# More word and stage places for the conversion of the second layer's inputs, home loads two positions apart, and other rules for the activation's jobs

## The chip, the core and the metric

One core of a Trainium2 chip. The metric is the device time of one execution in microseconds. Five engines work beside each other, each through its own queue in order: TensorE (PE, with its weight loads PEld), VectorE (DVE), ScalarE (ACT), GpSimd (POOL) and SyncE (SP). DMAs are issued here on SP's and ACT's queues.

## What is computed

An attention with feature maps (4 batches, 8 heads, 576 rows, 64 columns), whose output is laid out as 2304 tokens of 512, and then two layers of two products each. The second layer's inputs, and the first layer's weights, come as 64-bit floats.

```python
h = x @ w_in            # first layer: 2304 x 512 by 512 x 2048
g = np.maximum(0.01 * h, h)
x = (g @ w_out)         # 2048 x 512
h = x @ w_in            # second layer, weights of its own
sp = np.where(h > 20.0, h, np.log1p(np.exp(np.minimum(h, 20.0))))
g = h * np.tanh(sp)
out = (g @ w_out)
```

## The kernel before

The program runs through five stages: attention (to 180 us), the first layer's first product (to 352), its second product (352 to 575), the second layer's first product (575 to 772), and the last product (772 to 981). Every fp32 product is made of three matmuls (`three`, L97 to L100) on a high and a low part: `split` (L93 to L95) makes the high part on ScalarE (L94) and the low part on VectorE (L95). The second product of a layer runs in 72 steps of 12 matmuls, TensorE's operands being the weights at their *home* and the activations *gh*, *gl* (first layer) or *g* (second layer).

Beside TensorE's work a **planner** issues all other work. It is written in the kernel (`Stage`, `Chain`, `Lane`, `work`): each call of `work` is one *position*. It adds `rate` to a budget of VectorE time, and lets each active chain make its next stage if its gate is free, its places are there (`ok`), the stage before it is `after` positions old, and the budget is above zero. In the two second products a position stands behind each half step, so two positions to a step and six matmuls to a position. `work(True)` is a forced round, which looks neither at the budget nor at the age of a stage.

**Conversion of inputs.** 64-bit weights are loaded raw into a *stage* place (512 KB), and turned into fp32 on VectorE (L182, L184, L169, L197) and ScalarE (L190), in *word* places. `w2_chain` converts two such units of the second layer's input weights and stores their sums and parts to DRAM (`pd`, L1070); `to_parts` does it for a unit of its output weights (`po`, L985). A unit can only begin when a stage place has been loaded and two word places are open. In the first layer's second product the planner has two stage places and four word places; the tiles `s8` to `s13` of the first layer's inputs are out of use there until the second layer's inputs are made. In the last chunk of that product the code waits for the conversions:

```python
            if m == 3:
                free.add("u3")
                while any(x.tile is not None for x in places.stages) or loads.at < len(loads.units):
                    work(True)
```

It stands behind step 3 of the last 16 steps, with TensorE's next matmuls behind it in the program.

**The activation of the second layer** is done in 36 *jobs* (`job`, 128 x 1024 each): load `job<-hp` (L1370), exp (L1378), u, n (L1382, L1385), ln, exp (L1388, L1391), t1, t2 (L1394), t3 (L1405), t4 (L1409), store `gp<-job` (L1414). All but exp and ln are VectorE's. Jobs run in the lane `jobs`, four at a time, in tiles of the pool `wide`. They begin in the second layer's first product and go on to the end of the last one. `Pairs` loads their results as *raw* tiles (L1446) into three places in turn (`st0`, `st1`, `cc`), which until then serve jobs (`wide_at`, closed by `gates2`), and splits them: pair q, of 36, stands behind the first half of step 2q - 2 and is read from step 2q on.

**Home loads.** `to_home` loads the 16 last weights (`wo<-po`, 512 KB each, L1292) from DRAM to their homes. Eight wait for the gate `s0`, six for `s1`, two for `c1`; they are 16 chains, so those of a gate go at one position.

## Time and profile before

| | us |
|---|---|
| median of 3 runs | 986.84 (986.5 to 987.19) |
| the profiled execution | 987.44 |
| its span in the trace | 985.4 |
| TensorE busy | 927.7 (94%) |
| VectorE busy | 746.8 (76%) |
| ScalarE busy | 562.8 (57%) |
| GpSimd busy | 68.7 (7%) |
| DMA, whole span | 221.38 MB, 225 GB/s |

The time of the profiled execution is its span and 2.0 us around it. The page cuts the span into 40 slices of 24.6 us: a digit is the busy share in tenths, and PEclk the granted clock of TensorE in tenths of full speed. In the list of waits the engine and line that waited stand left of the arrow, what ended the wait right of it. In a timeline, a number in brackets is the idle time ahead of the instruction and what ended it.

### The profile page before, as it was taken

The numbers are of one execution on the slowest core, as the hardware profiler recorded it, in microseconds if no ns is written. First come the engines' busy times: TensorE is split into PE (matmuls) and PEld (weight loads), VectorE is DVE, ScalarE is ACT, GpSimd is POOL, SyncE is SP. The second block draws the span as 40 slices with busy tenths as digits, with TensorE's granted clock in tenths as the row PEclk, the third lists the DMA queues.
The fourth block names the chain that finished last, engine by engine and source line by source line (L and its number), as shares of the span: only waits on it lengthen the run. The fifth ranks groups of instructions, "written<-read, shape, count | busy, mean of one in ns | idle before, by whom it ended". The sixth has DMA issues, their size and how long they took to land.

```text
span 985.4 us, 17037 instructions
## 1 busy us (share of the span) xinstructions
PE 927.7 (94%) x6549; PEld 783.6 (80%) x6549; DVE 746.8 (76%) x1100; ACT 562.8 (57%) x869; POOL 68.7 (7%) x36
## 2 busy tenths in 40 slices
PE   8999999999999999999992899999999599999998
PEld 7899999788888888889881688787877488887886
DVE  7888987588888337776767696777877388888894
ACT  6788888555666445454443465464655346654461
POOL 3434442000000000000000000000000000000000
PEclk9999999999999999999996899999999899999999
DMA  7425521279887777887878646887888948565743
GB/s 202 132 75 143 140 61 31 101 237 308 301 284 263 259 233 236 268 282 255 266 249 266 242 155 226 288 294 267 303 284 309 415 161 298 192 236 192 237 169 128
DMA packets 126416, 221.38 MB, mean 225 GB/s; under 512 B 33664, under 2 KB 58624, under 8 KB 126336
## 3 DMA queue, kind: packets, MB, share of 16 engines
q1 hardware_dynamic: 89312, 144.40, 44.1%
q10 hardware_dynamic: 37024, 75.91, 22.0%
q8 instruction: 51, 0.84, 0.4%
q14 instruction: 29, 0.24, 0.1%
HBM read 131.66 MB, written 88.60 MB: 224 GB/s over the span
## 4 chain that ended last, share of the span: by engine, by line
PE 53%; DVE 14%; DMA 7%; issue 6%; ACT 6%; ACTq 0%; SPq 0%; DVEq 0%
PE a L98 8%; PE b L98 8%; PE a L100 8%; PE b L99 8%; PE b L100 8%; PE a L99 8%; DVE job L1394 3%; DVE job L1385 2%; DVE job L1405 2%; DMA wo<-po 2%; DVE g L95 2%; ACT job L1388 2%; DMA hp<-g 1%; DVE job L1409 1%; ACT job L1391 1%
## 5 line engine op out<-in xcount | busy, mean ns | idle before, releaser
L1394 DVE SCALAR_TENSOR_TENSOR job<-job 128x1024 f32<-128x1024 f32 x72 | 88.0, 1223 | 43.2 <-ACT job L1391 42.5
L1388 ACT ACTIVATE job<-job,two 128x1024 f32<-128x1024 f32 x36 | 41.5, 1152 | 93.8 <-DVE job L1385 91.3
L95 DVE TENSOR_TENSOR gl<-raw,gh 128x512 fp32r<-128x512 f32 x72 | 49.6, 691 | 59.6 <-ACT gh L94 56.4
L98 PE MATMUL b<-gh,wo 128*128 128x512 f32 (+1 forms) x192 | 68.9, 359 | 21.1 <-ACT gh L94 21.1
L94 ACT ACTIVATE gh<-raw 128x512 fp32r<-128x512 f32 x72 | 44.9, 627 | 62.0 <-PE a L100 15.7
L95 DVE TENSOR_TENSOR g<-raw,g 128x1024 fp32r<-128x1024 f32 x36 | 44.0, 1222 | 42.2 <-ACT g L94 40.8
L444 POOL PARTITION_ALL_REDUCE qm<-qd x32 | 68.5, 2188 | 91.0 <-ACT qd L439 82.3
L99 PE MATMUL b<-gl,wo 128*128 128x512 f32 (+1 forms) x192 | 69.0, 359 | 2.7 <-DVE gl L95 2.7
L98 PE MATMUL b<-wo,g 128*128 128x512 f32 x160 | 63.3, 395 | 6.7 <-ACT g L94 6.7
L100 PE MATMUL b<-gh,wo 128*128 128x512 f32 (+1 forms) x192 | 68.7, 358 | 0.0
L98 PE MATMUL b<-win,w 128*128 128x512 f32 x128 | 52.5, 410 | 12.3 <-DVE g L831 7.5
L100 PE MATMUL b<-wo,g 128*128 128x512 f32 x160 | 63.4, 396 | 0.5 <-DVE g L95 0.4
L99 PE MATMUL b<-wo,g 128*128 128x512 f32 x160 | 63.0, 394 | 0.0
L98 PEld LDWEIGHTS b<-gh,wo 128*128 128x128 f32 x192 | 36.9, 192 | 26.7 <-ACT gh L94 21.6
L94 ACT ACTIVATE g<-raw 128x1024 fp32r<-128x1024 f32 x36 | 37.4, 1049 | 35.2 <-DMA raw<-gp 24.0
L100 PE MATMUL a<-wo,g 128*128 128x512 f32 x128 | 50.2, 392 | 1.0 <-DVE g L95 1.0
L100 PE MATMUL b<-win,w 128*128 128x512 f32 x128 | 50.6, 395 | 0.3 <-DMA w<-pd 0.3
L98 PE MATMUL a<-wo,g 128*128 128x512 f32 x128 | 50.0, 391 | 0.7 <-ACT g L94 0.7
L99 PE MATMUL b<-win,w 128*128 128x512 f32 x128 | 50.4, 394 | 0.0
L99 PE MATMUL a<-wo,g 128*128 128x512 f32 x128 | 49.9, 390 | 0.0
L98 PE MATMUL a<-gh,wo 128*128 128x512 f32 x128 | 49.9, 390 | 0.0
L100 PE MATMUL a<-gh,wo 128*128 128x512 f32 x128 | 49.9, 389 | 0.0
(272 smaller groups left out, 2714.1 us busy)
## 6 DMA issues: line engine op xcount, KB each, us to landing
gd<-g ACTq DMA_DIRECT2D x72, 256.0 KB, 3.8
raw<-gd ACTq DMA_DIRECT2D x72, 256.0 KB, 3.7
hp<-g ACTq DMA_DIRECT2D x72, 256.0 KB, 3.6
job<-hp SPq DMA_DIRECT2D x36, 512.0 KB, 5.2
gp<-job SPq DMA_DIRECT2D x36, 512.0 KB, 3.0
raw<-gp ACTq DMA_DIRECT2D x36, 512.0 KB, 3.6
stage<-in_moe_w_in_dram SPq DMA_DIRECT2D x32, 512.0 KB, 4.5
stage<-in_moe_w_out_dram SPq DMA_DIRECT2D x32, 512.0 KB, 4.3
```

The source lines that it names most:

```text
L94: nc.scalar.activation(out=hi, in_=src, func=AF.Copy)
L95: nc.vector.tensor_tensor(out=lo, in0=src, in1=hi.bitcast(F32), op=ALU.subtract)
L98: nc.tensor.matmul(out=o, lhsT=wh_, rhs=xh, start=start, stop=False, **kw)
L99: nc.tensor.matmul(out=o, lhsT=wh_, rhs=xl, start=False, stop=False, **kw)
L100: nc.tensor.matmul(out=o, lhsT=wl_, rhs=xh, start=False, stop=stop, **kw)
L444: nc.gpsimd.partition_all_reduce(qm, qd, P, bass_isa.ReduceOp.absmax)
L1385: nc.vector.scalar_tensor_tensor(out=flat("e"), in0=flat("e"), scalar=E20, in1=flat("u"), op0=ALU.min, op1=ALU.mult)
L1388: nc.scalar.activation(out=flat("u"), in_=flat("e"), func=AF.Ln, bias=two)
L1391: nc.scalar.activation(out=flat("u"), in_=flat("u"), func=AF.Exp, scale=-1.0)
L1394: nc.vector.scalar_tensor_tensor(out=flat("t"), in0=flat(a), scalar=2.0, in1=flat(b), op0=op, op1=ALU.mult)
L1405: nc.vector.tensor_tensor(out=flat("t"), in0=flat("t"), in1=flat("e"), op=ALU.mult)
L1409: nc.vector.scalar_tensor_tensor(out=flat("t"), in0=flat("t"), scalar=-1.0, in1=flat("h"), op0=ALU.mult, op1=ALU.mult)
```

## The change

- In the first layer's second product `s10` and `s11` serve as four more word places and `s8` and `s9` as two more stage places, up to position 246.
- The stores of `w2_chain` (`put`) are issued two positions after their stage.
- The 16 home loads are one chain, two positions apart. The raw places `st0` and `st1` are closed to jobs one cycle earlier than before, `cc` as before.
- Up to six jobs run at a time, a job begins only while fewer than three are owed tiles, and only the oldest job's claim on tiles is kept free. A stage behind a ScalarE stage comes two positions later. The rates of the last two products are 1.38 and 0.95 instead of 1.4 and 0.96.

```diff
-        main, jobs = lanes = Lane(4), Lane(4, True)
+        main, jobs = lanes = Lane(4), Lane(6, True)
...
             def put(i):
-                def go():
+                def now():
                     pd[f, i] = dr.tile([P, 2, E if i == 1 else 2 * E], F32, name="pd%d_%d" % (f, i))
                     nc.sync.dma_start(out=pd[f, i], in_=part[i].bitcast(F32))
-                return go
+                return lambda: later(2, now)
...
-            chain(Stage(0.0, go, ("o",) + u, gate=gate_of(u)))
-
-        for u in out2:
-            to_home(u)
+            return Stage(0.0, go, ("o",) + u, gate=gate_of(u), after=2)
+
+        chain(*[to_home(u) for u in out2])
...
             def ok(force):
-                older = wants[:wants.index(left)] if left in wants else wants
-                return len(wide.open(wide.words)) - sum(x[0] for x in older) >= 1
+                rest = 0 if not wants or wants[0] is left else wants[0][0]
+                return len(wide.open(wide.words)) > rest
...
-                Stage(0.0, get, gate=("h",) + k, ok=ok), Stage(0.0, exp_, ok=ok, after=5), Stage(0.69, u_, ok=ok), Stage(1.22, n_),
-                Stage(0.0, ln_), Stage(0.0, r_), Stage(1.22, t1, ok=ok), Stage(1.22, t2), Stage(1.22, t3), Stage(1.22, t4),
+Stage(0.0, get, gate=("h",) + k, ok=lambda force: len(wants) < 3 and ok(force)), Stage(0.0, exp_, ok=ok, after=5), Stage(0.69, u_, ok=ok, after=2), Stage(1.22, n_),
+                Stage(0.0, ln_, after=2), Stage(0.0, r_), Stage(1.22, t1, ok=ok, after=2), Stage(1.22, t2), Stage(1.22, t3), Stage(1.22, t4),
...
-        s2 = Pairs()
+        s2, CLOSE3 = Pairs(), 246
...
+        for x in (10, 11):
+            t = place("s%d" % x, F32, 2, DM, pool=late[0], name="more")
+            places.words += [places.Word(lambda t=t, i=i: t[:, i], 0, CLOSE3) for i in range(2)]
+        for x in (8, 9):
+            places.stages.append(places.Word(lambda x=x: place("s%d" % x, I32, DM, 2, pool=late[0], name="stage"), 0, CLOSE3))
...
-        rate[0] = 1.4
+        rate[0] = 1.38
 
         def gates2(n):
+            if n == len(it) - 2:
+                for x in RAW2[:2]:
+                    wide_at[x].until = -1
             if n == len(it) - 1:
                 later(2, lambda: free.add("s0"))
-                for x in RAW2:
-                    wide_at[x].until = -1
+                wide_at[RAW2[2]].until = -1
...
-        rate[0] = 0.96
+        rate[0] = 0.95
```

What it does to the order, at three places. First VectorE at the waiting loop of the first layer's second product. `gl` is the low part of an activation, everything else here is conversion (`c`, `more`, `stage`, `wp` are its places and parts). Before, from the split ahead of the loop on:

```order
L95 TENSOR_TENSOR gl<-raw,gh 128x512
L257 TENSOR_TENSOR wp<-c,wp 128x256
L249 TENSOR_TENSOR c<-c 128x256 x4
L257 TENSOR_TENSOR wp<-c,wp 128x512
L197 SCALAR_TENSOR_TENSOR c<-c,more 128x512
L182 TENSOR_SCALAR c<-stage 128x512
L184 TENSOR_SCALAR stage<-stage 128x512
L169 SCALAR_TENSOR_TENSOR more<-stage 128x512
L257 TENSOR_TENSOR wp<-c,wp 128x512
L980 TENSOR_TENSOR c<-c 128x512
L182 TENSOR_SCALAR c<-stage 128x512
L184 TENSOR_SCALAR stage<-stage 128x512
```

Now, some 25 positions ahead of that step:

```order
L95 TENSOR_TENSOR gl<-raw,gh 128x512
L182 TENSOR_SCALAR c<-stage 128x512
L184 TENSOR_SCALAR stage<-stage 128x512
L169 SCALAR_TENSOR_TENSOR more<-stage 128x512
L197 SCALAR_TENSOR_TENSOR more<-more 128x512
L95 TENSOR_TENSOR gl<-raw,gh 128x512
L197 SCALAR_TENSOR_TENSOR c<-c,more 128x512
L182 TENSOR_SCALAR c<-stage 128x512
L184 TENSOR_SCALAR stage<-stage 128x512
L169 SCALAR_TENSOR_TENSOR more<-stage 128x512
L95 TENSOR_TENSOR gl<-raw,gh 128x512
```

The first piece goes on like this: 34 rows of conversion stand before the next `gl`. In the second there are at most five between two.

Second SP's queue at the seam of the last two products; `wo<-po` are home loads, `gp<-job` stores of finished jobs, `job<-hp` loads of new ones. Before, the first burst of eight and the start of the next:

```order
L1292 DMA wo_8461<-po_0_1_4424 128x1024
L1292 DMA wo_8463<-po_1_1_4502 128x1024
L1292 DMA wo_8465<-po_2_1_4536 128x1024
L1292 DMA wo_8467<-po_3_1_4668 128x1024
L1292 DMA wo_8469<-po_4_1_4692 128x1024
L1292 DMA wo_8471<-po_5_1_5017 128x1024
L1292 DMA wo_8473<-po_6_1_5420 128x1024
L1292 DMA wo_8475<-po_7_1_5443 128x1024
L1414 DMA gp_0_8499<-job 128x1024
L1292 DMA wo_8561<-po_8_1_5666 128x1024
```

Now:

```order
L1292 DMA wo_8442<-po_0_1_4424 128x1024
L1292 DMA wo_8468<-po_1_1_4502 128x1024
L1413 DMA gp_1_8483<-job 128x1024
L1292 DMA wo_8495<-po_2_1_4536 128x1024
L1292 DMA wo_8522<-po_3_1_4668 128x1024
L1292 DMA wo_8560<-po_4_1_4692 128x1024
L1413 DMA gp_0_8562<-job 128x1024
L1369 DMA job<-hp_0_8407 128x1024
L1292 DMA wo_8582<-po_5_1_5020 128x1024
L1369 DMA job<-hp_1_8467 128x1024
```

The loads are spread over 32 positions, and stores and loads of jobs stand between them. On ACT's queue the raw load of pair 1 now follows that of pair 0 directly; it stood behind the split of pair 0, 18 rows later.

Third VectorE at the end of the program: `g<-raw,g` is the split of a pair, L1394 is t1 or t2, L1405 t3, L1409 t4 of a job (L1393, L1404, L1408 in the new file). Before, from the split of pair 32 on:

```order
L95 TENSOR_TENSOR g_9908<-raw_9841,g_9907 128x1024
L1405 TENSOR_TENSOR job<-job 128x1024
L1409 SCALAR_TENSOR_TENSOR job<-job 128x1024
L1394 SCALAR_TENSOR_TENSOR job<-job 128x1024
L95 TENSOR_TENSOR g_9942<-raw_9880,g_9941 128x1024
L1394 SCALAR_TENSOR_TENSOR job<-job 128x1024
L1405 TENSOR_TENSOR job<-job 128x1024
L1409 SCALAR_TENSOR_TENSOR job<-job 128x1024
L95 TENSOR_TENSOR g_9975<-raw_9952,g_9974 128x1024
L95 TENSOR_TENSOR g_10007<-raw_9986,g_10006 128x1024
```

Now, from the same split on:

```order
L95 TENSOR_TENSOR g_9881<-raw_9818,g_9880 128x1024
L1408 SCALAR_TENSOR_TENSOR job<-job 128x1024
L1393 SCALAR_TENSOR_TENSOR job<-job 128x1024 x2
L95 TENSOR_TENSOR g_9917<-raw_9907,g_9916 128x1024
L1404 TENSOR_TENSOR job<-job 128x1024
L1408 SCALAR_TENSOR_TENSOR job<-job 128x1024
L1393 SCALAR_TENSOR_TENSOR job<-job 128x1024
L95 TENSOR_TENSOR g_9953<-raw_9942,g_9952 128x1024
L1393 SCALAR_TENSOR_TENSOR job<-job 128x1024
L1404 TENSOR_TENSOR job<-job 128x1024
L1408 SCALAR_TENSOR_TENSOR job<-job 128x1024
L95 TENSOR_TENSOR g_9988<-raw_9985,g_9987 128x1024
```

The two t4 that stood behind the split of pair 32 were those of jobs 34 and 35; now there are three, of jobs 33, 34 and 35, and the last stands behind the split of pair 34 instead of ahead of it.

## Rows read from the trace of the kernel before

**Rows 1.** The page: busy time of TensorE, its slices, its granted clock

```profile
PE 927.7 (94%) x6549; PEld 783.6 (80%) x6549; DVE 746.8 (76%) x1100; ACT 562.8 (57%) x869; POOL 68.7 (7%) x36
...
PE   8999999999999999999992899999999599999998
...
PEclk9999999999999999999996899999999899999999
```

**Rows 2.** TensorE's waits, whole span: for whom, us in total, times, longest

```profile
PE b L98 <- ACT gh L94: 21.1, 1, 21.1
PE b L98 <- DVE g L831: 7.5, 8, 4.1
PE b L98 <- ACT g L94: 6.7, 1, 6.7
```

**Rows 3.** By stretch: length, each engine's busy us, granted clock, DMA share, GB/s

```profile
core 0: us, PE busy (x) PEld busy (x) DVE busy (x) ACT busy (x) POOL busy (x), PEclk, DMA share, GB/s
220.00:320.00 100.00, 99.64 (x484) 83.84 (x483) 86.66 (x168) 60.95 (x109) 0.00 (x0) 1.00 0.86 287
365.00:515.00 150.00, 150.00 (x754) 128.23 (x753) 105.19 (x192) 73.07 (x129) 0.00 (x0) 1.00 0.79 261
519.40:550.00 30.60, 6.97 (x22) 5.00 (x21) 19.25 (x37) 12.47 (x20) 0.00 (x0) 0.61 0.71 234
575.50:751.00 175.50, 167.97 (x793) 137.14 (x792) 134.11 (x138) 101.00 (x137) 0.00 (x0) 0.99 0.73 256
751.00:790.00 39.00, 27.16 (x111) 21.23 (x110) 20.98 (x21) 15.37 (x20) 0.00 (x0) 0.87 1.03 411
790.00:965.00 175.00, 172.77 (x756) 141.09 (x755) 152.87 (x139) 91.90 (x98) 0.00 (x0) 1.00 0.60 208
```

**Rows 4.** TensorE one by one at the first hole: start, duration, matmul, [idle before]

```profile
520.74 0.39 PE L98 MATMUL b<-gh,wo 128*128 128x512 f32 x1
...
521.88 0.39 PE L100 MATMUL b<-gh,wo 128*128 128x512 f32 x1
543.41 0.80 PE L98 MATMUL b<-gh,wo 128*128 128x512 f32 x1 [21.14 <-ACT gh L94]
...
550.26 0.39 PE L98 MATMUL b<-gh,wo 128*128 128x512 f32 x1
```

**Rows 5.** VectorE one by one, in the first hole

```profile
528.01 0.43 DVE L182 TENSOR_SCALAR c<-stage 128x512 f32<-128x512 f32 x1 [5.69 <-DMA po<-c]
```

**Rows 6.** TensorE at the second hole; the home loads' count, size, median landing

```profile
767.93 0.50 PE L98 MATMUL b<-win,w 128*128 128x512 f32 x1 [4.10 <-DVE g L831]
...
784.73 0.79 PE L98 MATMUL b<-wo,g 128*128 128x512 f32 x1 [6.73 <-ACT g L94]
...
786.58 0.63 PE L98 MATMUL b<-wo,g 128*128 128x512 f32 x1
...
789.14 0.41 PE L98 MATMUL b<-wo,g 128*128 128x512 f32 x1
...
wo<-po SPq DMA_DIRECT2D x16, 512.0 KB, 8.9
```

**Rows 7.** The last operations of VectorE (L95 splits, L1409 is t4), then TensorE

```profile
960.85 1.23 DVE L1409 SCALAR_TENSOR_TENSOR job<-job 128x1024 f32<-128x1024 f32 x1
...
966.78 1.22 DVE L1409 SCALAR_TENSOR_TENSOR job<-job 128x1024 f32<-128x1024 f32 x1
969.19 1.23 DVE L95 TENSOR_TENSOR g<-raw,g 128x1024 fp32r<-128x1024 f32 x1 [1.19 <-ACT g L94]
975.07 1.23 DVE L95 TENSOR_TENSOR g<-raw,g 128x1024 fp32r<-128x1024 f32 x1 [4.66 <-ACT g L94]
...
965.73 0.39 PE L100 MATMUL b<-wo,g 128*128 128x512 f32 x1
...
971.17 0.39 PE L100 MATMUL b<-wo,g 128*128 128x512 f32 x1
...
976.61 0.39 PE L100 MATMUL b<-wo,g 128*128 128x512 f32 x1
```

More of the change, by code (lines that the diff above doesn't have):

```diff
@@ L1357, in take @@
                 if left[0] == 0:
-                    wants.remove(left)
+                    wants[:] = [x for x in wants if x is not left]
                 return box[i]
             def ok(force):
-                older = wants[:wants.index(left)] if left in wants else wants
-                return len(wide.open(wide.words)) - sum(x[0] for x in older) >= 1
+                rest = 0 if not wants or wants[0] is left else wants[0][0]
+                return len(wide.open(wide.words)) > rest
             def flat(i):
```

## The prediction, made before the result was known

> **What bounds the kernel now.** I read the page's busy line and its slices first [rows 1]: TensorE is busy for 94% of the span and its slices read 8 or 9 nearly everywhere, so only the holes can be won. There are two, slices 21 and 22 (a 2, then an 8 at a granted clock of 0.6 and 0.8) and slice 31 (a 5). The list of what TensorE waited for names them [rows 2]: one wait of 21.1 us for the high part of an activation, one of 6.7 us for the same kind of tile in the last product, and 7.5 us in eight pieces for VectorE's additions (L831), of which one piece is 4.1 us. All other waits are short. The table by stage [rows 3] shows that no other engine is full where the holes are: VectorE is busy 105 of 150 us ahead of the first hole and 19 of 31 us in it. In the second hole the DMA engines are full (share 1.03, 411 GB/s).
>
> The first hole: TensorE starts a matmul every 0.228 us (1.14 us for five, [rows 4]). From 521.88 to 550.26 us it starts ten where 2.3 us would do, so the hole costs **26.1 us**: the waits, and the matmuls after them at the lower of its two clock levels, 1.2 instead of 2.4 GHz (granted 0.61 over the stretch, [rows 3]). It is the place where the code calls the planner in a loop until every input of the second layer is converted: 16 rounds, counted out from the planner's rules, in which no matmul is issued. VectorE waits there too, once 5.69 us for a store that had to leave a word place [rows 5]. Latency fills the hole, not work.
>
> The second hole: 39 us at 751 to 790 hold 111 matmuls, 36 of them half as wide: 75 x 0.228 + 36 x 0.12 (estimate, half) = 21.4 us, so it costs 17.6 us; I take **17**, since one or two matmuls at the edges are counted in. Its two waits stand in [rows 6], with the 16 loads of the last weights (8.4 MB), whose median from issue to landing is 8.9 us.
>
> **The change, part by part.** *Places for conversions.* Four word places and two stage places more, until position 246. Counted out, all 26 conversions that are left at the start of this product (position 124) are then issued between positions 139 and 240, two positions to a step of TensorE, and the loop finds nothing to do: its 16 rounds go, with the 26.1 us. No instruction is added; the same VectorE work now stands between the splits of the activations. Is there room? VectorE's 105 us of 365 to 515 and 19 us of the hole make 124 us in some 154, 81%; the DMA's 261 GB/s x 150 us and 234 x 31 us make 46.4 MB in 154 us, 301 GB/s. The nearest row is the first layer's own conversion, 220 to 320 us, with VectorE at 87% and 287 GB/s: TensorE lost 0.4 us in 100 there [rows 3]. I add **0.6 us**, and 2.5 as the upper end; a gain is excluded, TensorE being busy for all 150 us. The cover is gone if VectorE has to wait at the head of its queue: behind it stand the splits that TensorE waits for.
>
> *The pd stores two positions later.* 32 stores on SP's queue, moved behind a few loads. They are read back some ninety positions later or more, so they cost nothing; should SP run late, the stage loads behind them do, which is the rival below.
>
> *Home loads two positions apart, and the first two raw places free one cycle earlier.* The 16 loads stood in bursts of 8, 6 and 2 on SP; now they stand at positions 386 to 416, with stores of finished jobs between them. Load m is issued nine positions, some 12 us, ahead of its use. A store waits for its job's last VectorE operation, and the home load behind it waits too: 2 to 3 us, which the 12 cover. On ACT's queue the load of pair 1, which TensorE waited 6.7 us for, now stands right behind that of pair 0, eight positions ahead of its split instead of beside it. What is left: the 16 loads and the other traffic (208 to 256 GB/s beside them, [rows 3], mean 232) are 8.4 + 9.3 = 17.7 MB in 40 us. At the 411 GB/s of the second hole that takes 43 us, so the last loads come 3 us late. I leave **3 of the 17 us**: a gain of 14. Ends: 17, if latency hides that, and 8, if the two waits of the additions stay.
> The page SBUF — State Buffer of the Trainium skill, in its summary of rules, reckons transfers between HBM and SBUF at about 358 GB/s. By that the 17.7 MB would need 49 us and come 9 us late, and the sum would be 969. The row of 411 GB/s is above it, so the trace does not agree, and I hold to the row.
>
> *Jobs: six at a time, each step behind a ScalarE step two positions later, at most two jobs still owed places when one begins; rates 1.38 and 0.95.* In the second layer's first product the order crowds: two stretches of 16 positions hold 21.6 us of planned VectorE work, 1.35 a position, where no such stretch held over 17.9 behind the first. With the two additions of a cycle (about 0.17) that is 1.52 against the 1.37 us that TensorE needs: 2 x 16 x 0.15 = 4.8 us worse. Against it, fewer operations wait for ScalarE: the short waits for L831, 3.4 us, could go. I take **0**, ends +4.8 and -3.4.
>
> *The end of the program.* This is where the change takes something back. The last pairs go the round: the job's last operation (t4), its store, its load, the high part on ScalarE, the low part (split) on VectorE. From the end of t4 to the end of the split this took 970.42 - 962.08 = 8.34 us and 976.30 - 968.00 = 8.30 us for pairs 34 and 35 [rows 7]. They landed just in time: 970.42 against TensorE's third matmul of pair 34 at 971.17, 976.30 against 976.61. In the new order each job ends one split later: t4 of job 33 stands between splits 32 and 33, t4 of 34 between splits 33 and 34, t4 of 35 between 34 and 35. VectorE takes them in that order, so each split waits out its round at the head, and the next job's operations stand behind it. On the clock of before: t4 of job 33 takes the place between two splits that job 34's had, one step (12 matmuls, 2.7 us) earlier, so split 33 ends at 970.42 - 2.7 = 967.7 against 965.73: 2.0 late. Two operations of 1.25 and a round: 967.7 + 2.5 + 8.3 = 978.5 against 971.17: 7.3 late. Three operations and a round: 978.5 + 3.75 + 8.3 = 990.6 against 976.61: **13.9 us** late. Waits of 5 and 6 us also take the clock: after the 6.73 us wait matmuls came at 0.43 us instead of 0.228 from 786.58 to 789.14 [rows 6]. I add **2**: 15.9 in all. Ends: 6, if VectorE runs 8 us further ahead of TensorE than before, and 18, if it lags as much as 2 us more.
>
> **The sum.** The profiled execution took 987.44 us (span 985.4 and 2.0 around it). 987.4 - 26.1 + 0.6 - 14 + 0 + 15.9 = 963.8. It lies 0.6 above the median of the runs shown, 986.84, so the forecast is **963 us**.
>
> **The rivals.** *The end costs nothing*: the last jobs run far enough ahead on VectorE that no split waits. For it: 13% of VectorE's time is idle even in the last product (153 of 175 us busy, [rows 3]). Against it: the order of the three t4 and splits makes the chain of 10.8 and 12.0 us a pair whatever the lead, where TensorE takes 5.4. 963 - 15.9 = 947, with 2 us of waits left 949; chance 0.13.
> *The home loads still collide*: mixed traffic moves less than the bursts did. From 220 to 320 us a share of 0.86 moved 287 GB/s [rows 3], 334 at a share of 1: then the 17.7 MB take 53 us and come 13 us late, 10 more than I left, part of it caught by the lead of 12 us: 963 + 7 = 970; chance 0.15. The Trainium skill's 358 GB/s (SBUF — State Buffer, summary of rules) would put it at 969.
> *The crowded stretches of the second layer's first product bind*: 963 + 4.8 and a fall of the clock, 969; chance 0.06.
> *The other side: the conversion's waits move into the product.* Place: VectorE's queue between positions 139 and 240. If conversions wait at its head for their input or for a word place to be stored, as one did for 5.69 us [rows 5], the splits behind them wait. VectorE has 154 - 124 = 30 us free there, so it decides from the sixth wait of this size; with ten of 26, 57 - 30 = 27 us spill onto TensorE and the kernel takes 963 + 27 = 990. Against it: ahead of the hole TensorE lost nothing in 150 us [rows 3], and there are now eight word places where there were four, and that wait was for lack of one. Chance 0.04.
> *The change doesn't do what it says*, the loop still turns: 963 + 26 = 989. The order speaks against it: where 34 rows stood on VectorE between two splits there are at most five. Chance 0.01.
>
> **How the numbers follow.** The forecast, all terms near their size, has 0.61. The range 951 to 975 holds it with its bounds (the end's cost down to 6, the gain at the second hole from 8 to 17, the crowded stretches), and the second and third rival; it leaves out the first, the fourth and the fifth, 0.18. About 0.2% is what a measurement of this kernel can tell from no change. Faster 0.94, same 0.01, slower 0.05.
>
> **What would show it.** In the profile after: no slice of TensorE at 2; no wait for the high part of an activation over 3 us near half the span; the home loads landing in under 8.9 us in the median and no wait over 3 us at the seam of the last two products; three growing waits for the high or low part in the last 45 us, 1 to 2, 5 and 6 us, the last split ending some 14 us behind. It is wrong if TensorE's waits between the first hole's place and its start grow, or if the last splits wait for nothing.

## The result, and the profile after

The changed kernel takes **952.26 us** in the median of four runs (951.47 to 953.28), the kernel before 987.02 (986.5 to 988.05) beside it: a ratio of 0.9647, 95% interval 0.963 to 0.9664. The forecast was 963, so the change gained 11 us more than the sum said. The profiled execution took 952.22 us, its span 950.2.

The page of the changed kernel, TensorE's busy time, slices and granted clock, against [rows 1]:

```profile
PE 924.0 (97%) x6549; PEld 784.8 (83%) x6549; DVE 746.6 (79%) x1100; ACT 562.9 (59%) x869; POOL 68.7 (7%) x36
...
PE   8999999999999999999999999999999899999986
...
PEclk9999999999999999999999999999999999999997
```

The 2 and the 5 are gone. A new low stands where there was none: the last two slices read 8 and 6. Its list of TensorE's waits, against [rows 2] (engine and line, what ended the wait, us in total, times, longest):

```profile
PE b L98 <- ACT g L94: 9.4, 3, 4.1
...
PE b L100 <- DVE g L95: 2.1, 4, 0.5
PE b L98 <- DVE g L831: 2.0, 1, 2.0
```

The wait of 21.1 us is gone, that for the additions has fallen from eight of 7.5 us to one of 2.0, and the high parts of the last product's splits (one wait at the seam, two at the end) are now the largest item. By stretch, against [rows 3]:

```profile
core 0: us, PE busy (x) PEld busy (x) DVE busy (x) ACT busy (x) POOL busy (x), PEclk, DMA share, GB/s
365.00:515.00 150.00, 150.00 (x754) 128.15 (x753) 130.49 (x242) 83.78 (x149) 0.00 (x0) 1.00 0.91 319
515.00:548.50 33.50, 33.50 (x150) 27.73 (x149) 22.18 (x25) 13.48 (x19) 0.00 (x0) 1.00 0.51 176
548.50:711.50 163.00, 162.75 (x793) 136.77 (x792) 131.25 (x135) 101.15 (x137) 0.00 (x0) 1.00 0.80 281
722.00:734.00 12.00, 10.01 (x47) 8.58 (x46) 6.60 (x8) 4.24 (x5) 0.00 (x0) 0.86 1.03 395
914.00:948.00 34.00, 23.91 (x74) 16.93 (x73) 11.88 (x11) 3.96 (x6) 0.00 (x0) 0.80 0.23 86
```

First row: VectorE does 130 us of work in the 150 that held 105, DMA moves 319 GB/s instead of 261, and TensorE is busy for 150.00 of 150. Third row: the same 793 matmuls of the second layer's first product that took 175.5 us take 163.0.

To compare stages I use one measure for every kernel: the time from the start of one matmul to the start of another, counted in program order, less 0.2267 us for each matmul of 512 columns between them and 0.12 for each half as wide, TensorE's steady pace in these traces. What is left is what TensorE lost there, by waits and by its clock. The stages are cut at the same matmuls in every kernel. The second layer's first product ends here ahead of its last 71 matmuls, at 711.9 us of the changed kernel. The *seam* is these 71 and the last product into its pair 12, to 803.4 us:

| TensorE lost, us, in one profiled execution | before | after |
|---|---|---|
| first layer's second product, to the first hole | 0.5 | 0.3 |
| the place of the first hole | 26.2 | 0.0 |
| second layer's first product | 14.0 | 1.5 |
| seam of the last two products | 17.7 | 9.4 |
| last product, to pair 32 | 3.2 | 0.0 |
| pairs 33 to 35 | 0.0 | 15.7 |

The last row is the chain of the last jobs. VectorE of the changed kernel there, from the split of pair 34 to that of pair 35, and TensorE beside it:

```profile
924.93 1.23 DVE L95 TENSOR_TENSOR g<-raw,g 128x1024 fp32r<-128x1024 f32 x1 [5.86 <-ACT g L94]
926.07 1.22 DVE L1393 SCALAR_TENSOR_TENSOR job<-job 128x1024 f32<-128x1024 f32 x1
927.32 1.23 DVE L1404 TENSOR_TENSOR job<-job 128x1024 f32<-128x1024 f32 x1
928.58 1.23 DVE L1408 SCALAR_TENSOR_TENSOR job<-job 128x1024 f32<-128x1024 f32 x1
937.09 1.23 DVE L95 TENSOR_TENSOR g<-raw,g 128x1024 fp32r<-128x1024 f32 x1 [7.28 <-ACT g L94]
```

```profile
914.33 0.50 PE L98 MATMUL b<-wo,g 128*128 128x512 f32 x1
...
915.59 0.50 PE L100 MATMUL b<-wo,g 128*128 128x512 f32 x1 [0.53 <-DVE g L95]
...
924.95 0.80 PE L98 MATMUL b<-wo,g 128*128 128x512 f32 x1 [4.07 <-ACT g L94]
925.54 0.63 PE L99 MATMUL b<-wo,g 128*128 128x512 f32 x1
926.21 0.80 PE L100 MATMUL b<-wo,g 128*128 128x512 f32 x1
...
937.11 0.50 PE L98 MATMUL b<-wo,g 128*128 128x512 f32 x1 [3.44 <-ACT g L94]
938.37 0.79 PE L100 MATMUL b<-wo,g 128*128 128x512 f32 x1 [0.52 <-DVE g L95]
```

Split 34 waits 5.86 us at the head of VectorE's queue; behind it stand three operations of job 35, whose result split 35 needs; their end (929.81) to the end of split 35 (938.32) is 8.5 us, in which VectorE only waits (7.28 us) and then makes the split. From split to split 12.16 us pass, where [rows 7] had 5.88.

### The profile page after: what moved, and what is told of

Its sections match the earlier page's. It is cut to its first block, busy times and chain, and to the rows that moved or that the text cites. A ratio compares the mean times of both kernels' runs of the same rounds, so it can differ in the third digit from the quotient of the medians.

```text
span 950.2 us, 16996 instructions
## 1 busy us (share of the span) xinstructions
PE 924.0 (97%) x6549; PEld 784.8 (83%) x6549; DVE 746.6 (79%) x1100; ACT 562.9 (59%) x869; POOL 68.7 (7%) x36
## 4 chain that ended last, share of the span: by engine, by line
PE 69%; DMA 7%; DVE 5%; ACT 3%; issue 2%; ACTq 1%; DVEq 0%; SPq 0%
PE a L98 12%; PE a L100 12%; PE a L99 12%; PE b L100 10%; PE b L98 10%; PE b L99 10%; DMA gp<-job 2%; DMA raw<-gp 2%; PE outs L484 1%; DVE job L1393 1%; DVE g L95 1%; DVE job L1408 1%; DVE job L1404 1%; DMA wo<-po 1%; PE kvp L461 1%
## 5 line engine op out<-in xcount | busy, mean ns | idle before, releaser
L1393 DVE SCALAR_TENSOR_TENSOR job<-job 128x1024 f32<-128x1024 f32 x72 | 87.7, 1221 | 10.4 <-ACT job L1390 6.8
L95 DVE TENSOR_TENSOR g<-raw,g 128x1024 fp32r<-128x1024 f32 x36 | 44.0, 1223 | 47.6 <-ACT g L94 47.5
L95 DVE TENSOR_TENSOR gl<-raw,gh 128x512 fp32r<-128x512 f32 x72 | 49.6, 690 | 34.0 <-ACT gh L94 29.6
L98 PE MATMUL b<-wo,g 128*128 128x512 f32 x160 | 65.9, 412 | 9.4 <-ACT g L94 9.4
L100 PE MATMUL b<-wo,g 128*128 128x512 f32 x160 | 65.9, 412 | 2.1 <-DVE g L95 2.1
L1377 ACT ACTIVATE job<-job 128x1024 f32<-128x1024 f32 x36 | 37.9, 1055 | 47.8 <-DMA job<-hp 38.9
L99 PE MATMUL b<-wo,g 128*128 128x512 f32 x160 | 64.8, 405 | 0.0
L98 PE MATMUL b<-win,w 128*128 128x512 f32 x128 | 50.6, 395 | 2.2 <-DVE g L831 2.0
L100 PE MATMUL b<-win,w 128*128 128x512 f32 x128 | 50.0, 391 | 0.0
L99 PE MATMUL b<-win,w 128*128 128x512 f32 x128 | 50.0, 390 | 0.0
L99 PE MATMUL a<-gl,wo 128*128 128x512 f32 x128 | 49.8, 389 | 0.0
L98 PE MATMUL a<-wo,g 128*128 128x512 f32 x128 | 49.8, 389 | 0.0
L99 PE MATMUL a<-wo,g 128*128 128x512 f32 x128 | 49.8, 389 | 0.0
```

The lines of the kernel that those rows point to most:

```text
L95: nc.vector.tensor_tensor(out=lo, in0=src, in1=hi.bitcast(F32), op=ALU.subtract)
L98: nc.tensor.matmul(out=o, lhsT=wh_, rhs=xh, start=start, stop=False, **kw)
L99: nc.tensor.matmul(out=o, lhsT=wh_, rhs=xl, start=False, stop=False, **kw)
L100: nc.tensor.matmul(out=o, lhsT=wl_, rhs=xh, start=False, stop=stop, **kw)
L1377: nc.scalar.activation(out=flat("e"), in_=flat("h"), func=AF.Exp)
L1393: nc.vector.scalar_tensor_tensor(out=flat("t"), in0=flat(a), scalar=2.0, in1=flat(b), op0=op, op1=ALU.mult)
```

## The experiments

The lines shown are those in which each differs from the changed kernel (- is the changed kernel); ... stands for lines left out, which the text names. Losses are in the measure of the table above, each from the one profiled execution of the kernel.

**One: the places alone.** Taken back are the job rules, the rates, the stores two positions later, the spread home loads and the earlier closing of two raw places; only the word and stage places stay.

```diff
-        main, jobs = lanes = Lane(4), Lane(6, True)
+        main, jobs = lanes = Lane(4), Lane(4, True)
...
-                return lambda: later(2, now)
+                return now
...
-        chain(*[to_home(u) for u in out2])
+        for u in out2:
+            to_home(u)
...
-        rate[0] = 0.95
+        rate[0] = 0.96
```

> Only the places for the conversions: four more word places and two more stage places up to position 246; home loads, pd stores, job rules and rates as before. Theory: the parts act each in its own stage, so the first hole goes (26 us) and nothing else moves: 961 us, VectorE still waits some 40 us for ScalarE in the second layer's first product, TensorE still loses 12 to 14 us there and 17 us at the seam of the last two products, nothing at the end. Rival 1, the conversion's work is only passed on to the product it now lies beside: 970 or more. Rival 2, the conversion that ends earlier is also what cleared the second layer's first product: 948.

960.34 us (959.84 to 960.83), ratio 0.9734 (0.972 to 0.9749). The first hole costs 0, TensorE loses 13.3 us in the second layer's first product, 17.4 at the seam, 3.1 in the last product and 0.0 at the end: before's losses, all but the hole. So the places give 26.6 us and nothing else, and the conversion costs TensorE some 1 us beside its product (1.6 against 0.5).

**Two: without the gaps.**

```diff
-Stage(0.0, get, gate=("h",) + k, ok=lambda force: len(wants) < 3 and ok(force)), Stage(0.0, exp_, ok=ok, after=5), Stage(0.69, u_, ok=ok, after=2), Stage(1.22, n_),
-                Stage(0.0, ln_, after=2), Stage(0.0, r_), Stage(1.22, t1, ok=ok, after=2), Stage(1.22, t2), Stage(1.22, t3), Stage(1.22, t4),
+Stage(0.0, get, gate=("h",) + k, ok=lambda force: len(wants) < 3 and ok(force)), Stage(0.0, exp_, ok=ok, after=5), Stage(0.69, u_, ok=ok), Stage(1.22, n_),
+                Stage(0.0, ln_), Stage(0.0, r_), Stage(1.22, t1, ok=ok), Stage(1.22, t2), Stage(1.22, t3), Stage(1.22, t4),
```

> The change without the gap of two positions behind a ScalarE stage (u, ln and t1 come one position later again); six jobs at a time, the claim rules, the rates, places and home loads stay. Theory: the gap is what keeps VectorE from standing at the head of its queue for ScalarE. Without it VectorE's wait for the second exp in the second layer's first product returns from 7 to about 40 us and TensorE's lost time there from 2 to 10 to 14 us; the jobs end earlier, no t4 stands close ahead of its split, and the 16 us at the end go: 952 + 12 - 16 = 948. Rival, the six jobs and the claim rules cleared that product: TensorE loses 2 us there as now, and the end is free: 936.

954.02 us (953.69 to 955.58), ratio 0.9675 (0.9659 to 0.9692). The two effects are there and nearly cancel: 16.3 us lost in the first product instead of 1.5, 0.0 at the end instead of 15.7. The first was larger than I expected, so the total misses by 6. The way there was not the expected one either. In that product VectorE's waits for the second exponential come back to 13.8 us, not to 40; ScalarE's waits for n (L1384) come to 18.9, where they were 31.7 before and are 3.6 in the change; and TensorE waits longest for a copy that ScalarE makes (L781), not for an addition:

```profile
DVE job L1393 <- ACT job L1390: 13.8, 7, 6.7
...
ACT job L1387 <- DVE job L1384: 18.9, 12, 2.6
...
PE b L98 <- ACT b L781: 4.9, 6, 1.7
```

So without the gap VectorE and ScalarE wait for each other at the heads of both queues. How much of TensorE's loss hangs on which queue was not tried apart.

**Three: the home loads in bursts again**, and the raw places closed at the old cycle.

```diff
-            return Stage(0.0, go, ("o",) + u, gate=gate_of(u), after=2)
-
-        chain(*[to_home(u) for u in out2])
+            chain(Stage(0.0, go, ("o",) + u, gate=gate_of(u)))
+
+        for u in out2:
+            to_home(u)
...
-            if n == len(it) - 2:
-                for x in RAW2[:2]:
-                    wide_at[x].until = -1
...
-                wide_at[RAW2[2]].until = -1
+                for x in RAW2:
+                    wide_at[x].until = -1
```

> The change with the home loads in bursts of 8, 6 and 2 again and the three raw places closed together again; everything else as changed. Theory: the spreading is what the seam of the last two products gained, 8 us (17 before, 9 after): 960, the home loads' median landing back at 9 us. Rival, the raw load of pair 1 comes early by the job rules and the bursts hurt no more than the spread loads: within 2 us of 952.

956.80 us (956.19 to 957.33), ratio 0.9698 (0.9684 to 0.9713): spreading them and closing two places earlier are together worth 4.5 us, half of what I expected. The seam costs 14.6 instead of 9.4. TensorE in this kernel, its two waits of over 1 us there:

```profile
727.19 0.65 PE L98 MATMUL b<-win,w 128*128 128x512 f32 x1 [4.27 <-DVE g L831]
...
747.25 0.50 PE L98 MATMUL b<-wo,g 128*128 128x512 f32 x1 [3.65 <-ACT g L94]
```

The same two of the changed kernel:

```profile
724.74 0.50 PE L98 MATMUL b<-win,w 128*128 128x512 f32 x1 [1.99 <-DVE g L831]
...
742.11 0.50 PE L98 MATMUL b<-wo,g 128*128 128x512 f32 x1 [1.85 <-ACT g L94]
```

Both waits are half as long with the loads spread, in these two executions, and neither is gone; the other kernels with spread loads that were profiled show 2.3 to 4.7 us for the first, but for twelve, which has none.

**Four: the last three splits half a pair later** in VectorE's queue, behind two operations of the next job.

```diff
-                while self.split_at <= min((s + 1) // 2 + 1, NS // 2 - 1):
+                while self.split_at <= min((s + (1 if self.split_at < NS // 2 - 3 else 0)) // 2 + 1, NS // 2 - 1):
```

> The change with one thing moved: the splits of the last three pairs stand half a pair (one step of TensorE) later, so that the next job's t3 and t4 stand ahead of the split of pair 33 and t1 to t3 of the last job ahead of that of pair 34. Jobs, rates and loads stay where they are. Theory: the end's loss is the chain of rounds on VectorE's queue, each split waiting at the head with the next job's operations behind it; with the chain cut, only the last pair is late, by about 4 us instead of 16: 941. Rival, the jobs simply end too late (the rate is too low) and a split that stands later is later: 952 to 955.

943.52 us (943.15 to 944.28), ratio 0.9565 (0.9551 to 0.9579). The end costs 6.0 instead of 15.7 (I expected 4), with no operation added or taken away. That the order on VectorE made the chain is shown.

**Five: without the job rules and rates**, all else as in the change.

```diff
-        main, jobs = lanes = Lane(4), Lane(6, True)
+        main, jobs = lanes = Lane(4), Lane(4, True)
...
-                rest = 0 if not wants or wants[0] is left else wants[0][0]
-                return len(wide.open(wide.words)) > rest
+                older = wants[:wants.index(left)] if left in wants else wants
+                return len(wide.open(wide.words)) - sum(x[0] for x in older) >= 1
...
-Stage(0.0, get, gate=("h",) + k, ok=lambda force: len(wants) < 3 and ok(force)), Stage(0.0, exp_, ok=ok, after=5), Stage(0.69, u_, ok=ok, after=2), Stage(1.22, n_),
...
+Stage(0.0, get, gate=("h",) + k, ok=ok), Stage(0.0, exp_, ok=ok, after=5), Stage(0.69, u_, ok=ok), Stage(1.22, n_),
...
-        rate[0] = 0.95
+        rate[0] = 0.96
```

> The change with its rules for the activation's jobs taken back (four at a time, the old rule for places, no steps two positions apart, rates 1.40 and 0.96); word and stage places, stores and spread home loads stay. Theory: the job rules alone cleared the second layer's first product and alone made the chain at the end. Against the change TensorE loses some 11 us again in the first product (before: 12.4, there 1.5), some 3 in the body of the last product, and gets the 15.8 at the end back: 952.3 + 11 + 3 - 15.8 = 951, with VectorE waiting over 35 us for ScalarE's second exponential. Rival: the spread home loads or the places cleared the first product, not the rules: then only the end changes and it takes 937 to 940.

959.71 us (958.71 to 960.5), ratio 0.9726 (0.9708 to 0.9744), 9 us over the theory's 951. Its first half holds: 13.3 us lost in the first product. Its second does not: pairs 33 to 35 still lose 5.1, the pairs ahead of them 3.1, and the seam 10.5. Set beside experiment one, which has the same job rules: with the loads spread and two places closed earlier the seam lost 6.9 us less (17.4 to 10.5), and 5.1 of them came back at the end, where one had lost nothing. The last two jobs are stored 7 and 6 positions ahead of use in five, 8 and 7 in one, and with that difference t4 of job 35 stands behind the split of pair 34 instead of ahead of it. VectorE in five, then in one:

```profile
937.68 1.23 DVE L95 TENSOR_TENSOR g<-raw,g 128x1024 fp32r<-128x1024 f32 x1 [2.36 <-ACT g L94]
938.82 1.22 DVE L1408 SCALAR_TENSOR_TENSOR job<-job 128x1024 f32<-128x1024 f32 x1
```

```profile
940.11 1.22 DVE L1409 SCALAR_TENSOR_TENSOR job<-job 128x1024 f32<-128x1024 f32 x1
942.49 1.23 DVE L95 TENSOR_TENSOR g<-raw,g 128x1024 fp32r<-128x1024 f32 x1 [1.15 <-ACT g L94]
```

The order's part is at most the wait of 2.36 us ahead of that t4. The rest I read as lead: TensorE begins pair 33 6.5 us earlier in five (932.08 and 938.61), and VectorE ends job 35 only 1.3 us earlier (940.04 and 941.33). That reading is argued from these two runs, not tried apart.

**Six: the rate of the last product at 1.0.**

```diff
-        rate[0] = 0.95
+        rate[0] = 1.0
```

> The change with one number different: the rate of the last product is 1.0 instead of 0.95, so that the last three jobs are stored 12, 11 and 10 positions ahead of their use instead of 6, 5 and 4. Theory: the end of the program is lost to the order alone, since each of the last splits waits out a round through DRAM with the next job's operations behind it; with ten positions (some 13 us) ahead the round of 8.3 us is covered, the 15.8 us go and the kernel takes 936 to 938, nothing else being touched. Rival: VectorE has no time left, and a higher rate on paper only moves the waits into the body of the last product: 945 or more.

941.36 us (938.87 to 943.16), ratio 0.9547 (0.9524 to 0.957), 3 to 5 over the theory. In the profiled execution, the fastest of the four (938.87), the end costs 0.0 and the body 0.5; what is over lies at the seam, 12.0 us against 9.4. VectorE in this kernel, from the end of job 35 on:

```profile
913.19 1.22 DVE L1408 SCALAR_TENSOR_TENSOR job<-job 128x1024 f32<-128x1024 f32 x1
918.63 1.23 DVE L95 TENSOR_TENSOR g<-raw,g 128x1024 fp32r<-128x1024 f32 x1 [4.22 <-ACT g L94]
921.67 1.22 DVE L95 TENSOR_TENSOR g<-raw,g 128x1024 fp32r<-128x1024 f32 x1 [1.81 <-ACT g L94]
```

The last job is done 8.5 us ahead of the end of the split that needs it (914.41 to 922.89), two splits of waiting are left, and no operation stands behind them. One number of the planner was worth 11 us.

**Seven: a gap of one, a rate of 0.98 and the later splits**, all in the last product.

```diff
-Stage(0.0, get, gate=("h",) + k, ok=lambda force: len(wants) < 3 and ok(force)), Stage(0.0, exp_, ok=ok, after=5), Stage(0.69, u_, ok=ok, after=2), Stage(1.22, n_),
...
+Stage(0.0, get, gate=("h",) + k, ok=lambda force: len(wants) < 3 and ok(force)), Stage(0.0, exp_, ok=ok, after=5), Stage(0.69, u_, ok=ok, after='gap'), Stage(1.22, n_),
...
-        rate[0] = 0.95
+        rate[0] = 0.98
+        gap[0] = 1
...
-                if pos[0] < self.at + x.after and not force:
+                if pos[0] < self.at + (gap[0] if x.after == 'gap' else x.after) and not force:
```

The other two gaps alike, and the split's line of experiment four.

> The change with three edits in the last product: steps behind a ScalarE step come one position later instead of two, the rate is 0.98, and the last three splits stand half a pair later in VectorE's queue. The last jobs are stored 15, 10 and 9 positions ahead of their use. Theory of the round trip: the end loss goes as with the rate alone, 936 to 938. Rival: the shorter gap brings VectorE's waits for ScalarE back in the last product, as before the change, where its body lost some 3 us: 940 or more.

942.05 us (940.33 to 943.25), ratio 0.9546 (0.9525 to 0.9568): the rival's time. The body of the last product loses 5.1 us, the end 1.1. Which of the three edits costs the body its 5 was not separated, and VectorE's waits for the second exponential are only 1.6 us there, so the rival's reason isn't shown.

**Eight: six, and pair 2 loaded earlier.** All three raw places are closed to jobs one cycle earlier.

```diff
-                for x in RAW2[:2]:
+                for x in RAW2:
...
-                wide_at[RAW2[2]].until = -1
...
-        rate[0] = 0.95
+        rate[0] = 1.0
```

> The change with the rate of the last product at 1.0, and all three raw places closed to jobs one cycle earlier (the change does so for two): the load of pair 2 is issued seven positions earlier, ahead of most home loads. Theory: what is left at the seam of the last two products (about 9 us) is half one load that comes late, that of pair 2, issued with that of pair 3 behind six home loads, and the clock that falls after the wait of 2.0 us; without it the kernel takes 3 to 4 us less than with the rate alone. Rival: the transfers are at their limit there, so the wait goes to another tile (pair 3, or an addition) and the time is within 1 us of the rate alone; or the place that the jobs miss makes the last jobs later again (8, 7 and 6 positions ahead) and the end loses 2 to 3 us.

939.99 us (938.21 to 940.64), ratio 0.9524 (0.9505 to 0.9543); the interval overlaps that of six. In the traces the seam costs 5.7 instead of 12.0, and the end 4.6 instead of 0.0, with the last jobs stored 8, 7 and 6 positions ahead of their use instead of 12, 11 and 10. The stretch from 734 to 750 us, first six, then eight:

```profile
734.00:750.00 16.00, 15.47 (x67) 12.23 (x66) 11.84 (x12) 8.63 (x9) 0.00 (x0) 1.00 1.02 397
```

```profile
734.00:750.00 16.00, 16.00 (x72) 13.25 (x71) 13.55 (x13) 9.55 (x10) 0.00 (x0) 1.00 1.02 389
```

With the DMA engines as full, TensorE now waits for nothing in those 16 us. So what was late there was one load behind six others, not the sum of the transfers. But of the 6.3 us at the seam only 1.1 lie there, in pairs 1 to 3; 4.8 lie in pairs 4 to 12, and why was not followed. In pairs 1 to 3 the change lost 4.5 us, and all four kernels that load pair 2 early (eight, nine, eleven, twelve) lose 0.0.

**Nine: eight, at a rate of 1.05.**

```diff
-                for x in RAW2[:2]:
+                for x in RAW2:
...
-                wide_at[RAW2[2]].until = -1
...
-        rate[0] = 0.95
+        rate[0] = 1.05
```

> All three raw places closed one cycle earlier, as in e8, and the rate of the last product at 1.05: the last three jobs are stored 13, 12 and 12 positions ahead of their use (8, 7 and 6 in e8). Theory: the two gains add once the last jobs keep ten positions; the 4.6 us that e8 lost in its last three pairs go, the seam stays as there, 940.0 - 4.6 = 935.4. Rival: a job place fewer and a higher rate press VectorE's waits into the body of the last product, 939 or more.

**935.15 us** (933.87 to 936.03), ratio 0.9476 (0.9461 to 0.9491). As expected: the end 0.0, the body 0.0, the seam 6.9. It is the fastest of all, 17 us under the change.

**Ten: experiment five with the gaps given back** (four jobs at a time, the old rule for places).

```diff
-        main, jobs = lanes = Lane(4), Lane(6, True)
+        main, jobs = lanes = Lane(4), Lane(4, True)
...
-        rate[0] = 1.38
+        rate[0] = 1.4
```

> e5 (the change without its job rules) with one rule given back: steps behind a ScalarE step two positions later; four jobs at a time, the old rule for places and the old rates stay. Theory: the gap alone clears the second layer's first product: there TensorE loses 2 us instead of the 13 of e5, and VectorE's waits for the second exponential fall from 46 to under 10 us. Fewer jobs then end in time: fourteen forced rounds stand in the last product, pairs 28 to 35 are stored 4 to 8 positions ahead of their use, and eight splits wait out a round of 5 to 7 us each over TensorE's 5.4: 960 - 11 + 30 = 980, with 960 to 990 possible. Rival: without six jobs at a time the gap only moves the waits to another step, and the first product still loses 8 us or more.

980.89 us (980.11 to 982.32), ratio 0.9942 (0.9927 to 0.9957). The first product loses 0.1 us, the last product to pair 32 40.4, pairs 33 to 35 9.8. VectorE's waits for the second exponential in the first product fall with the loss; before, then five, then the change, then ten (where the longest of its kind is now for the first exponential):

```profile
DVE job L1394 <- ACT job L1391: 40.5, 16, 4.9
```

```profile
DVE job L1393 <- ACT job L1390: 41.7, 16, 6.7
```

```profile
DVE job L1393 <- ACT job L1390: 6.8, 4, 3.7
```

```profile
DVE job L1381 <- ACT job L1377: 9.1, 4, 3.8
...
DVE job L1393 <- ACT job L1390: 1.5, 2, 1.2
```

So the gap clears the first product, whichever of four or six jobs run. The six jobs and the new rules for places together pay for the gap: without them the jobs fall behind, until TensorE waits 34.7 us for the splits of the last product.

**Eleven: nine with the later splits of four.** The diff is that of nine and that of four.

> e9 with the last three splits half a pair later in VectorE's queue, as in e4. Theory: with 12 positions ahead the round is covered whichever side of the next job's step a split stands, so it is within 1 us of e9. Rival: VectorE runs late enough that the order still counts, and it is 2 us or more faster than e9; or the later splits are themselves late for TensorE, and it is 2 us slower.

938.24 us (936.48 to 940.3), ratio 0.9511 (0.9494 to 0.9529), 3 us slower than nine, and I had expected no difference. From pair 12 on this kernel loses 3.2 us, 1.9 of them at the start of pair 33, where nine loses nothing. The place is ScalarE's queue; its rows from the load of the next raw pair on:

```profile
907.48 6.01 ACTq L1445 DMA_DIRECT2D raw<-gp  x2
913.59 2.01 ACT L94 ACTIVATE g<-raw 128x1024 fp32r<-128x1024 f32 x2 [10.75 <-DMA gp<-job]
```

The later split now stands behind the second of two raw loads, whose issue takes 6.0 us together; what ScalarE was released by, in brackets, is a job's store, which that load reads back. What helped where VectorE was late (four) hurts where it is not.

**Twelve: nine with the split of pair 0 behind the last addition but one**, not ahead of it. The lines that differ from nine:

```diff
-            then.splits(-3)
+            if few:
+                then.splits(-3)
```

> e9 with the split of pair 0 of the last product two positions later: it stood ahead of the last addition but one (L831) of the second layer's first product in VectorE's queue, now it stands right behind it. Theory: in e9 VectorE waits 5.1 us at that split for its high part, with the addition behind it, and TensorE waits 2.3 us for the addition, then runs eighteen half-wide matmuls at the lower clock, 0.215 us instead of 0.12; the last 4 us of the seam are this order and no transfer, and they go: 935.2 - 4 = 931, with a granted clock of 1.0 throughout the seam. Rival: the split is what is really late, and TensorE waits for pair 0 at the start of the last product instead: within 1 us of e9.

936.46 us (934.59 to 938.18), ratio 0.9491 (0.9477 to 0.9506): the rival. The seam costs 7.9 us against 6.9. (The half-wide matmuls behind the wait in nine are twelve, not eighteen.) In nine, VectorE and then TensorE at the seam:

```profile
723.74 1.23 DVE L95 TENSOR_TENSOR g<-raw,g 128x1024 fp32r<-128x1024 f32 x1 [5.06 <-ACT g L94]
724.88 0.68 DVE L831 TENSOR_TENSOR g<-b,z 128x512 f32<-128x512 f32 x1
```

```profile
725.62 0.50 PE L98 MATMUL b<-win,w 128*128 128x512 f32 x1 [2.31 <-DVE g L831]
```

In twelve ScalarE, then TensorE:

```profile
726.79 0.33 ACTq L1332 DMA_DIRECT2D hp<-g  x1
727.16 1.06 ACT L1390 ACTIVATE job<-job 128x1024 f32<-128x1024 f32 x1 [2.96 <-DMA wo<-po]
...
728.60 1.05 ACT L94 ACTIVATE g<-raw 128x1024 fp32r<-128x1024 f32 x1
```

```profile
729.70 0.50 PE L98 MATMUL b<-wo,g 128*128 128x512 f32 x1 [2.65 <-ACT g L94]
```

The addition no longer waits, and pair 0 does. ScalarE stood 2.96 us, by the trace until a home load landed, behind a store that it issues itself, and the high part of pair 0 behind that. So what is left at the seam may hang on the full transfers after all, through ScalarE's queue; what held the store's issue was not tried, and this is not shown.

## Why the prediction was right, and where it missed

The time fell inside the range, 1 us above its lower end; the sum was 11 us too high. That the range held it is partly luck: the gain of the job rules lies far outside the ends of its own term, and only the seam's miss the other way, 5.7 us, kept the time above 951. Term by term, from the profiled 987.44 to 952.22 us:

| term | predicted | measured |
|---|---|---|
| first hole | -26.1 | -26.2 |
| conversion beside the product | +0.6 | -0.2 |
| second hole, the seam | -14 (-17 to -8) | -8.3 |
| job rules, second layer's first product | 0 (-3.4 to +4.8) | **-12.5** |
| last product, to pair 32 | not in the sum | -3.2 |
| end of the program | +15.9 (6 to 18) | +15.7 |

What is left, -0.5, lies ahead of the first layer's second product.

*The first hole* went as the step said. The two profiled executions give -0.2 for the conversion; the kernels with the places vary between 0.3 and 1.6 lost there, so the 0.6 can't be told from them.

*The job rules were the step that failed.* I took them at 0, with a gain of 3.4 at most, since I counted only TensorE's waits for one line (L831) in one list. The stage itself was the place to read. It lost 14.0 us before (in [rows 3], TensorE idle for 7.5 of 175.5, the rest in matmuls slower than the pace), and its mark stood in VectorE's list of waits, which I had not set against the gap: 40.5 us in 16 waits for ScalarE's second exponential, at the head of a queue that also holds the additions for TensorE. That the gap clears this product is shown (two and ten). That VectorE's queue alone is the way is not: in two its waits are a third of that, 13.8 us, ScalarE waits 18.9 for VectorE, and TensorE loses more, 16.3. The crowding that I weighed against it, +4.8, did not bind: 0.25 us idle in 163.

*The seam* came out 5.7 us short of the term, near its lower end. The reason given, that 17.7 MB take 43 us and come 3 us late, is not shown to be what cost it. The home loads did land sooner, 7.8 us in the median instead of 8.9, and no wait at the seam was over 3 us, as the prediction said; but nine, with 9.0, lost less there than the change. Two waits stayed, at half their size or less, each for one tile that stood badly in a queue: pair 2's load behind the home loads (gone in eight, at the same DMA rate), and the split of pair 0 with an addition behind it (twelve moved its wait, and did not remove it).
The page SBUF — State Buffer of the Trainium skill, in its summary of rules, reckons about 358 GB/s between HBM and SBUF. The stretches of 395 GB/s above, and of 389 with TensorE waiting for nothing, do not agree. The page HBM Reference of the Trainium skill, under Specifications (TRN2), says that a core streaming alone measures well above the per-core share, about 425 GB/s. With that the rows agree: they lie between the two figures.

*The end of the program* was right in its mechanism and its size. Pairs 33, 34 and 35 were to be 2.0, 7.3 and 13.9 us late; against TensorE's pace from 914.33 on, its third matmuls were 0.8 (915.59 for 914.78), 6.0 (926.21 for 920.2) and 12.7 late (938.37 for 925.7): the steps of 5.3 and 6.6 hold, and VectorE ran 1.2 us further ahead than I took. The clock after the last wait cost 3.0 instead of 2.

*The body of the last product*, 3.2 us that I did not price: it is nearly gone without the gaps too (0.4 in two) and stands at 3.1 in one and five, so it seems to hang on how many jobs run, on the rules for places or on the rates, which all differ there. Which of them was not tried; six jobs and the new rules alone are no guard, since seven has both and lost 5.1.

Of the rivals, the home loads did still collide, with about the loss given (9.4 us at the seam, where 3 were left and 7 more feared), but not for its reason: mixed traffic was to move 334 GB/s at a full share, and the stretches above moved 389 to 397. The loss was paid for by a gain elsewhere. "The end costs nothing" was wrong for this kernel and is what one number in the rate makes true (six).

## What to carry to other kernels

When an edit moves work within an in-order queue, look at the waits at the heads of all queues in the stage, and price it by what the bound engine loses in that stage as a whole: its own list names only what came last (7.5 us idle of 14.0 lost), and the waits of the others are no measure of the loss (40.5 us of VectorE's beside 14.0, 13.8 beside 16.3). Work that ends in a round through DRAM should stand a full round ahead of its use, with nothing of the next round behind the wait; where that was so here, the same work was free (15.7 us and 0.0, by a rate of 0.95 or 1.0). And time won in one stage may shorten the lead of the work beside it, as one and five suggest, so look at the end of the program again after each gain.

## What the hardware showed

- The round of a 512 KB tile (store, load, high part, low part) took 8.5 us from the end of t4 to the end of the split, in the change and in experiment six; [rows 7] give 8.3.
- After the waits of 4.1 and 3.4 us at the end matmuls stand at 0.63 to 0.80 us each in the rows above, where the steady ones show 0.39, with a granted clock of 0.80 over 914 to 948 us: part of the time at 1.2 GHz, the lower of its two levels. The four waits shown are 8.6 of the 15.7 us lost; the rest, nearly as much again, is matmuls slower than the pace.
- From the first to the end of the second of two loads' issues on ScalarE's queue 6.0 us passed, by the trace until a store was done that one of them reads (eleven), and ScalarE's own work stood behind it.
